# The late score matmuls issued as two instruction groups: the pooled rounds with six dense blocks a head first, the other dense blocks a few groups later

## The chip, the cores and the metric

The kernel runs on one core of one Trainium2 chip, in one launch. The metric is device time in microseconds (us). TensorE (PE) multiplies, VectorE (DVE) and ScalarE (ACT) read its results from PSUM, GpSimd (POOL) works between SBUF tensors, and SyncE (SP) issues the DMAs.

## What is computed

For 8 batches with 8 heads, 576 positions and 64 features per head, two attentions are added, and the sum goes through a token-mixing step of rank 32 and a feed-forward network (FFN) of width 2048:

```python
q_d, k_d, v_d = (t.reshape(B, H, S // 4, 4, D).mean(axis=3) for t in (q, k, v))
out_up = np.repeat(sm_attn(q_d, k_d, v_d), 4, axis=2)      # pooled: softmax over 144 x 144
mask = np.abs(pos[:, None] - pos[None, :]) < 4             # local: 7 keys for each query
scores = np.where(mask, scale * q @ k.T, -1e9)
x = out_up + softmax(scores) @ v                           # heads side by side: (B, S, 512)
u = x + (x.transpose(0, 2, 1) @ U @ V).transpose(0, 2, 1)
out = u + np.maximum(u @ w_ch1, 0.0) @ w_ch2
```

(The softmax and the transposes are shortened here.) All arithmetic is in 32 bits; the FFN splits each operand into a high and a low part (uH, uL, W1H, W1L and so on) and adds three products.

## The kernel before

**Work and names.** The FFN takes 256 steps, one for each batch, half of the positions (288) and block of 128 hidden features. A step is twelve matmuls into `ps_h` (line 888), a Relu on ACT into `hH` (L895), the rest `hL` on DVE (L896), and three steps later twelve matmuls into four `acc` tiles (L911). Below, "a group" is twelve FFN matmuls. Attention runs for two heads at a time, called a pair here. The first five pairs take an early path; the other 27 take the late path, which is where the change is. Between FFN groups a late pair puts five kinds of work on PE: the scores `ps_b` (L719 and L726), the transposes `ps_t` (L539), the weighted sums `ps_a` (L552), the mixing `ps_hu` (L848) and `ps_u` (L863).

**The scores of a late pair.** Two PSUM tiles, one for each head, are 128 partitions by 512 columns. Partitions 0 to 71 hold in columns 114 to 401 the pooled scores (`pooled_view`). The dense blocks, 32 queries by 38 keys each, are the local scores: three for each of the first three groups of 32 partitions, in columns 0 to 113, and nine for the last group, in columns 0 to 341. The function `mm` issues all 48 passes of both heads in one run: the first pooled half with three dense blocks of the last group beside it, twelve blocks of all groups, the second pooled half with the last three blocks. Passes on different groups of 32 output partitions, and on the two heads' halves of 64 input partitions, run side by side in PE's array.

**Who reads them.** The pooled part goes to a maximum `mx` on DVE (L520), its negative `nb` on ACT (L522) and four exponentials `E` on ACT (L525); then come the transposes, the sums and a store `up_s`. The dense part goes to four copies `se` on ACT (L744), a store to DRAM `s_s`, a reload `sc`, the local softmax (`ms` on DVE, L770, and what follows), the products `Pt` on POOL (L799) and their sums on DVE (L804).

**What sets the order.** All work is first recorded as operations with an engine, an assumed duration, buffers and a priority. `Plan.run` then places them in assumed time, on each engine the ready operation with the lowest priority number first, and emits the instructions in that order; each engine runs its own in order. FFN groups have numbers from 1000 up, attention work below 320, so attention goes first when the plan holds it ready. A latency `lat` is added between an operation and those that need it. Semaphore waits are added afterwards by the layer under the kernel, by buffer: for a PSUM tile, an instruction waits for the accesses by other engines to the same tile that stand ahead of it in the emitted order, whichever columns they touch. So a DVE maximum may wait for an ACT copy of the same tile, and a later PE pass into it waits for both. PSUM tiles of a late pair's scores, transposes and sums share one tag with two buffers.

**The first 236 us.** W1 and W2 are converted on the core from 64-bit to 32-bit parts, five instructions on ACT and DVE and one on POOL for each block of 512 columns (`c`, `w1r`, `w2r`, W1H, W2L; lines 341 to 354), while the FFN of batch 0 and the attention of batch 1 already run.

Of the kernel before, what the change touches and what calls it, by code (L numbers as in the profile page):

```python
# [15 lines left out]
AF = mybir.ActivationFunctionType  # L16
ALU = mybir.AluOpType
AX = mybir.AxisListType
# [3 lines left out]
PE, DVE, ACT, POOL, SP = range(5)  # L22
SLACK_FROM = 80
SLACK = 0.0
MARGIN, MARGIN_FROM = (0.5,0.0,0.0,0.0,0.0), 50
LATENCY = (0.2, 0.15, 0.2, 0.2, 0.95)


class Buf:
# [24 lines left out]
class Plan:  # L54
# [6 lines left out]
    def buf(self, pool, shape, dt, name, tag=None, bufs=1):  # L61
        return Buf(self, pool, shape, dt, name, tag or name, bufs)

    def op(self, eng, dur, fn, r=(), w=(), prio=0.0, after=(), lat=None, move=0.0, at=0.0):
        o = Op()
        o.eng, o.dur, o.fn, o.prio, o.succ, o.ndep, o.ready = eng, dur, fn, prio, [], 0, at
        o.lat, o.move = LATENCY[eng] + SLACK * (SLACK_FROM <= prio < 1000) if lat is None else lat, move
        deps = set(after)
# [133 lines left out]
def attn_mix_ffn_kernel(ctx: ExitStack, tc, q, kp, vp, qT, kT, v, U, Ub, V, w1, w2, mask, band, eye, pat, pool, vw, vn, ident, outT):  # L202
# [25 lines left out]
    QL, KL = 32, 38  # L228
# [8 lines left out]
    op, buf = plan.op, plan.buf  # L237
# [82 lines left out]
    for _ in range(2):  # L320
        m = kept_tile([NS, 2, KW], "ms_b")
        op(POOL, 0.4, lambda m=m: nc.gpsimd.tensor_copy(
            out=m()[:, :, :, KL:KW].rearrange("p r h k -> p (r h) k"),
            in_=pat_sb.unsqueeze(1).broadcast_to([128, 2 * NS, KW - KL])), ["pat"], [(m, "pat")], 0.1)
# [170 lines left out]
    def late_global(b, hp, up_s, prio):  # L495
        h0 = 2 * hp
        g = lambda shape, name, bufs=1: buf(glo, shape, F32, name, None, bufs)
        sq, sk = g([128, SD], "smq"), g([128, SD], "smk")
        qr, kr = g([128, S], "gq"), g([128, SPAD], "gT")
        load_t(qr, qT, b, h0, prio)  # L500
        load_t(kr, kT, b, h0, prio)
        pool_halves(qr, 0, sq, False, prio)
        pool_halves(kr, (SPAD - S) // 2, sk, False, prio)
        vss = []
        for hh in range(2):
            x, vs = g([QH, 2, 4, D], "vr"), g([QH, 2, D], "vs", 2)
            vss.append(vs)
            dma(lambda hh=hh, x=x: nc.sync.dma_start(
                out=x(), in_=v[b, h0 + hh].rearrange("(a p r) d -> p a r d", a=2, r=4)), [], [x], prio, 150)
            pool_tt(256, lambda x=x: nc.gpsimd.tensor_tensor(  # L510
                out=x()[:, :, 0:2, :], in0=x()[:, :, 0:2, :], in1=x()[:, :, 2:4, :], op=ALU.add), [x], [x], prio)
            pool_tt(128, lambda x=x, vs=vs: nc.gpsimd.tensor_tensor(
                out=vs(), in0=x()[:, :, 0, :], in1=x()[:, :, 1, :], op=ALU.add), [x], [vs], prio)
        s_s = buf(dram, [2, S, KL + 1], F32, "s_s", bufs=4)
        ps = late_scores(qr, kr, sq, sk, s_s, prio - 0.4)
        rs, rr, ri = (g([QH, 4], n) for n in ("rs", "rr", "ri"))
        Es = [g([QH, 2, SD], "E", 2) for _ in range(2)]
        for hh in range(2):
            mx, nb = g([QH, 2], "mx", 2), g([QH, 2], "nb", 2)
            dve(288, lambda hh=hh, mx=mx: nc.vector.tensor_reduce(  # L520
                out=mx(), in_=pooled_view(ps[hh]), axis=AX.X, op=ALU.max), [ps[hh]], [mx], prio)
            act(2, lambda mx=mx, nb=nb: nc.scalar.activation(  # L522
                nb(), mx(), AF.Copy, scale=-1.0 / 128.0), [mx], [nb], prio, 0.16)
            for a in range(2):
                act(SD, lambda a=a, hh=hh, nb=nb: nc.scalar.activation(  # L525
                    Es[hh]()[:, a, :], pooled_view(ps[hh])[:, a], AF.Exp, bias=nb()[:, a:a + 1], scale=1.0 / 128.0,
                    accum_out=rs()[:, 2 * hh + a:2 * hh + a + 1]), [ps[hh], nb], [(Es[hh], a), (rs, a, hh)], prio, 0.237)
        act(4, lambda: nc.scalar.activation(rr(), rs(), AF.Copy, bias=4e-9, scale=4.0),
            [(rs, a, hh) for a in range(2) for hh in range(2)], [rr], prio, 0.16)
        dve(24, lambda: nc.vector.reciprocal(out=ri(), in_=rr()), [rr], [ri], prio)  # L530
        ek = [(E, a) for E in Es for a in range(2)]
        view = lambda t: t()[:QH, :2 * SD].rearrange("p (c q) -> p c q", c=2)
        pt = psum_pair(ps_m, "ps_t", "m:g", 2)

        def t_mm():
            for hh in range(2):
                for c in range(2):
                    for a in range(2):
                        nc.tensor.transpose(view(pt[hh])[:, c, a * QH:(a + 1) * QH],  # L539
                                            Es[hh]()[:, a, c * QH:(c + 1) * QH], ident_sb[:QH, :QH])  # L540
        op(PE, 0.52, t_mm, ek + ["ident"], pt, prio)
        for hh in range(2):
            act(288, lambda hh=hh: nc.scalar.activation(Es[hh](), view(pt[hh]), AF.Copy),
                [pt[hh]], [(Es[hh], 0), (Es[hh], 1)], prio, 0.05)
        pa = psum(ps_m, "ps_a", "m:g", 2)
        out = lambda: pa()[:QH, :4 * D].rearrange("p (a d) -> p a d", a=4)

        def a_mm():
            for hh in range(2):
                for a in range(2):  # L550
                    for c in range(2):
                        nc.tensor.matmul(out()[:, 2 * hh + a, :], Es[hh]()[:, c, a * QH:(a + 1) * QH],  # L552
                                         vss[hh]()[:, c, :], start=(c == 0), stop=(c == 1))
        op(PE, 1.06, a_mm, ek + vss, [pa], prio)
        od = g([QH, 4, D], "od")
        dve(256, lambda: nc.vector.tensor_tensor(
            out=od(), in0=out(), in1=ri().unsqueeze(2).broadcast_to([QH, 4, D]), op=ALU.mult), [pa, ri], [od], prio)

        def store(hh):
            for a in range(2):  # L560
                nc.sync.dma_start(
                    out=up_s()[hh, a * QH * 4:(a + 1) * QH * 4, :].rearrange("(p r) d -> p r d", r=4),
                    in_=od()[:, 2 * hh + a, :].unsqueeze(1).broadcast_to([QH, 4, D]))
        for hh in range(2):
            dma(lambda hh=hh: store(hh), [od], [(up_s, hh)], prio, 160, 0.85)
        return s_s
# [143 lines left out]
    HB, LB = 3, NL - 9  # L710
    pooled_view = lambda t: t()[:QH, HB * KL:HB * KL + 2 * SD].rearrange("p (a k) -> p a k", a=2)

    def late_scores(qr, kr, sq, sk, s_s, prio):
        ps = psum_pair(ps_m, "ps_b", "m:g", 2)

        def dense(c, r):
            n = HB * c + r
            for hh, o in enumerate(heads):
                nc.tensor.matmul(ps[hh]()[c * QL:(c + 1) * QL, r * KL:(r + 1) * KL], qr()[o, n * QL:(n + 1) * QL],  # L719
                                 kr()[o, n * QL:n * QL + KL], start=True, stop=True)  # L720

        def pooled(a):
            for c in range(3):
                m = slice(c * QL, min((c + 1) * QL, QH))
                for hh, o in enumerate(heads):
                    nc.tensor.matmul(ps[hh]()[m, HB * KL + a * SD:HB * KL + (a + 1) * SD],  # L726
                                     sq()[o, a * QH + m.start:a * QH + m.stop], sk()[o], start=True, stop=True)

        def mm():
            pooled(0)  # L730
            for r in range(3):
                dense(3, r)
            for r in range(HB):
                for c in range(3):
                    dense(c, r)
                dense(3, 3 + r)
            pooled(1)
            for r in range(6, LB):
                dense(3, r)
        op(PE, 1.1, mm, [qr, kr, sq, sk], ps, prio)  # L740
        for hh in range(2):
            se = buf(loc, [128, LB, KL], F32, "se", bufs=2)
            for n, rows in ((HB, slice(0, 3 * QL)), (LB, slice(3 * QL, 4 * QL))):
                act(n * KL, lambda p=ps[hh], se=se, n=n, rows=rows: nc.scalar.activation(  # L744
                    se()[rows, 0:n].rearrange("p r k -> p (r k)"), p()[rows, 0:n * KL], AF.Copy), [ps[hh]], [(se, n)], prio)

            def put(hh=hh, se=se):
                for c in range(4):
                    n = HB if c < 3 else LB
                    to = s_s()[hh, HB * c * QL:(HB * c + n) * QL, :]  # L750
                    dst = bass.AP(tensor=to.tensor, offset=to.offset, ap=[[KL, QL], [QL * (KL + 1), n], [1, KL]])
                    nc.sync.dma_start(out=dst, in_=se()[c * QL:(c + 1) * QL, 0:n])
            dma(put, [(se, HB), (se, LB)], [(s_s, hh)], prio, 100, 1.7)
        return ps
# [296 lines left out]
```

## Time and profile before

| what | value |
|---|---|
| three runs | 1033.8, 1037.79, 1038.47 us; median 1037.79 |
| the profiled execution | 1038.36 us; its span on the core is 1036.6 us |
| mean granted TensorE clock | 0.981 |
| busy share PE, DVE, ACT, POOL | 96%, 51%, 37%, 54% |

The profiled execution is 0.57 us above the median of the three runs. 1.76 us of it lie outside the span, before the first and after the last instruction. Busy PE counts overlapping matmuls once, and their ends are modelled; so how dense PE's work is must be read from starts, not from busy time.

### The profile page before, as it was taken

To read this page: it belongs to the slowest core of one execution; us is meant where nothing else is said; L and a number is where in the kernel's file an instruction comes from. 1 tells how busy PE (TensorE), PEld (TensorE's weight loads), DVE (VectorE), ACT (ScalarE), POOL (GpSimd) and SP (SyncE) were. 2 spreads that over 40 slices of the span, in tenths; PEclk is the share of its full clock that TensorE was granted. 3 is DMA by queue.
4 is the path that set the end of the run, shared out by engine and by line. 5 is a ranking of instruction groups with operands and counts; after the bars stand their busy time and mean duration, and the time that the engine had idled before them with its cause. 6 is when DMAs were issued, how large, how long until landed. Compare 5 with 4: busy or idle time off the path is not lost.

```text
span 1036.6 us, 26946 instructions
## 1 busy us (share of the span) xinstructions
PE 996.9 (96%) x10831; PEld 975.3 (94%) x10831; DVE 529.8 (51%) x1054; ACT 388.0 (37%) x1234; POOL 557.2 (54%) x567
## 2 busy tenths in 40 slices
PE   6778898999999999999999999999999999999998
PEld 5667888999999999999999999999999999999998
DVE  5997898655554545444475344534652544211111
ACT  3676554442443434443344244423443232111110
POOL 4854568788575656565585638762765625211010
PEclk9896999999999999999999999999999999999999
DMA  8866764753555545545555355624644242000000
GB/s 279 226 172 179 199 186 116 149 138 104 135 137 115 141 113 132 128 86 146 120 137 125 87 132 133 143 75 101 151 116 117 64 113 50 24 1 24 1 24 23
DMA packets 222612, 120.30 MB, mean 116 GB/s; under 512 B 175492, under 2 KB 198456, under 8 KB 222488
## 3 DMA queue, kind: packets, MB, share of 16 engines
q1 hardware_dynamic: 222488, 118.58, 45.5%
q8 instruction: 85, 1.39, 0.6%
q14 instruction: 39, 0.32, 0.1%
HBM read 87.78 MB, written 30.75 MB: 114 GB/s over the span
## 4 chain that ended last, share of the span: by engine, by line
PE 84%; DVE 7%; POOL 3%; issue 2%; DMA 2%; ACT 2%; SPq 0%; DVEq 0%; POOLq 0%; ACTq 0%
PE acc L911 36%; PE ps_h L888 35%; PE ps_a L552 2%; PE ps_b L719 2%; DVE c L347 2%; PE ps_hu L848 1%; DVE c L349 1%; PE ps_t L539 1%; DMA w2r<-in_W 1%; PE ps_b L726 1%; POOL Pt L799 1%; DVE c L342 1%; DVE c L344 1%; PE ps_a L484 1%; PE ps_v L431 1%
## 5 line engine op out<-in xcount | busy, mean ns | idle before, releaser
L911 PE MATMUL acc<-hH,W2H 128*128 128x288 f32 x1024 | 310.5, 303 | 0.0
L896 DVE SCALAR_TENSOR_TENSOR hL<-ps_h,hH 128x288 fp32r<-128x288 f32 x256 | 116.6, 455 | 378.6 <-ACT hH L895 378.0
L888 PE MATMUL ps_h<-uH,W1H 128*128 128x288 f32 x1024 | 304.3, 297 | 4.1 <-DVE hL L896 3.1
L911 PE MATMUL acc<-hH,W2L 128*128 128x288 f32 x1024 | 303.1, 296 | 2.6 <-POOL W2L L354 2.6
L888 PE MATMUL ps_h<-uL,W1H 128*128 128x288 f32 x1024 | 303.4, 296 | 1.2 <-POOL uL L871 1.2
L911 PE MATMUL acc<-hL,W2H 128*128 128x288 f32 x1024 | 302.6, 296 | 0.0
L888 PE MATMUL ps_h<-uH,W1L 128*128 128x288 f32 x1024 | 302.0, 295 | 0.0
L799 POOL TENSOR_TENSOR Pt<-vl,at 128x896 f32<-128x896 f32 (+1 forms) x135 | 233.4, 1809 | 115.1 <-DVE acc L804 61.1
L895 ACT ACTIVATE hH<-ps_h 128x288 fp32r<-128x288 f32 x256 | 105.1, 410 | 433.6 <-PE ps_h L888 433.5
L888 PEld LDWEIGHTS ps_h<-uH,W1H 128*128 128x128 f32 x1024 | 193.5, 189 | 5.4 <-DVE hL L896 3.8
L911 PEld LDWEIGHTS acc<-hH,W2L 128*128 128x128 f32 x1024 | 193.2, 189 | 3.5 <-POOL W2L L354 3.5
L888 PEld LDWEIGHTS ps_h<-uL,W1H 128*128 128x128 f32 x1024 | 193.4, 189 | 1.5 <-POOL uL L871 1.5
L911 PEld LDWEIGHTS acc<-hH,W2H 128*128 128x128 f32 x1024 | 193.3, 189 | 1.1
L888 PEld LDWEIGHTS ps_h<-uH,W1L 128*128 128x128 f32 x1024 | 193.7, 189 | 0.0
L911 PEld LDWEIGHTS acc<-hL,W2H 128*128 128x128 f32 x1024 | 193.7, 189 | 0.0
L804 DVE TENSOR_REDUCE acc<-Pt 128x128 f32<-128x1024 f32 (+1 forms) x135 | 144.7, 1103 | 4.7 <-POOL Pt L799 2.3
L871 POOL TENSOR_TENSOR uL<-xT,uH 128x288 fp32r<-128x288 f32 x56 | 44.1, 811 | 71.3 <-ACT uH L869 71.2
L921 POOL TENSOR_TENSOR o<-uH,uL 128x288 f32<-128x288 f32 x64 | 49.8, 816 | 54.2 <-DMA out_t<-o 54.2
L840 POOL TENSOR_TENSOR xL<-xL,xH 116x640 fp32r<-116x640 f32 x28 | 44.0, 1572 | 64.2 <-ACT xH L839 49.3
L510 POOL TENSOR_TENSOR vr<-vr 72x256 f32<-72x256 f32 x54 | 42.4, 785 | 46.9 <-DMA vr<-in_v 46.8
L793 ACT ACTIVATE Pt<-ul 128x128 f32<-128x128 f32 (+1 forms) x135 | 48.4, 441 | 21.3 <-DVE acc L804 20.0
L744 ACT ACTIVATE se<-ps_b 96x114 f32<-96x114 f32 x108 | 38.5, 357 | 47.1 <-PE ps_b L719 34.1
(129 smaller groups left out, 1106.9 us busy)
## 6 DMA issues: line engine op xcount, KB each, us to landing
vl<-in_vp SPq DMA_DIRECT2D x54, 240.0 KB
out_t<-o SPq DMA_DIRECT2D x64, 144.0 KB
w1r<-in_W SPq DMA_DIRECT2D x16, 512.0 KB
w2r<-in_W SPq DMA_DIRECT2D x16, 512.0 KB
Y<-x_s SPq DMA_DIRECT2D x112, 72.0 KB
gT<-in_kT SPq DMA_DIRECT2D x27, 291.0 KB
xL<-x_s SPq DMA_DIRECT2D x28, 280.0 KB
gq<-in_qT SPq DMA_DIRECT2D x27, 288.0 KB
```

Of the source, the lines that this page charges most:

```text
L510: pool_tt(256, lambda x=x: nc.gpsimd.tensor_tensor(out=x()[:, :, 0:2, :], in0=x()[:, :, 0:2, :], in1=x()[:, :, 2:4, :], op=ALU.add), [x], ...
L744: act(n * KL, lambda p=ps[hh], se=se, n=n, rows=rows: nc.scalar.activation(se()[rows, 0:n].rearrange("p r k -> p (r k)"), p()[rows, 0:n * ...
L793: act(n * D, lambda n=n, ps=ps, Pt=Pt: nc.scalar.activation(Pt()[:, :n, :, 7], ul()[:, ps, :], AF.Copy), [ul], [(Pt, 1)], prio, 0.16)
L799: nc.gpsimd.tensor_tensor(out=Pt()[:, :n, :, 0:7].rearrange("p s d o -> p o s d"), in0=win, in1=at()[:, ps, :].rearrange("p s o -> p o s") ...
L804: dve(8.5 * n * D, lambda n=n, ps=ps, Pt=Pt: nc.vector.tensor_reduce(out=acc()[:, ps, :], in_=Pt()[:, :n], axis=AX.X, op=ALU.add), [(Pt, 0 ...
L840: pool_tt(640, lambda: nc.gpsimd.tensor_tensor(out=xL(), in0=xL().bitcast(F32), in1=xH().bitcast(F32), op=ALU.subtract), [xL, xH], [xL], prio)
L871: pool_tt(TN, lambda uH=uH, uL=uL, uf=uf: nc.gpsimd.tensor_tensor(out=uL()[:, hp, :], in0=uf(), in1=uH()[:, hp, :].bitcast(F32), op=ALU.su ...
L888: nc.tensor.matmul(ps()[:, :TN], w[:, dc, fs], u()[:, dc, :], start=(n == 0), stop=(n == 3 * NDC - 1))
L895: last_h[i] = act(TN, lambda: nc.scalar.activation(hH(), ps()[:, :TN], AF.Relu), [ps], [hH], FIRST, 0.05)
L896: dve(TN, lambda: nc.vector.scalar_tensor_tensor(hL(), ps()[:, :TN], 0.0, hH().bitcast(F32), op0=ALU.max, op1=ALU.subtract), [ps, hH], [hL ...
L911: nc.tensor.matmul(ac[e]()[:, :TN], W2[w][:, fc, es], hx(), start=(fc == 0 and n == 0), stop=(fc == NFC - 1 and n == 2))
L921: pool_tt(TN, lambda e=e, o1=o1: nc.gpsimd.tensor_tensor(out=o1()[:, :TN], in0=uH()[:, e, :].bitcast(F32), in1=uL()[:, e, :].bitcast(F32), ...
```

## The change

The 48 passes are recorded as two operations in place of one. The first, `first`, holds both pooled halves and six dense blocks of the last partition group of each head; the second, `rest`, holds the other twelve blocks of each head. `rest` needs `first` and 1.2 us (`RUN_GAP`) after it in the plan's time. The maximum and the exponentials need `first` alone; the copies `se` need both. The assumed durations add up to what they were (0.65 + 0.45 = 1.1 us). No pass is added or taken away.

```diff
+RUN_GAP = 1.2
...
-                out=mx(), in_=pooled_view(ps[hh]), axis=AX.X, op=ALU.max), [ps[hh]], [mx], prio)
+                out=mx(), in_=pooled_view(ps[hh]), axis=AX.X, op=ALU.max), [(ps[hh], 0)], [mx], prio)
...
-        def mm():
-            pooled(0)
-            for r in range(3):
-                dense(3, r)
+        def first():
+            for a in range(2):
+                pooled(a)
+                for r in range(3 * a, 3 * a + 3):
+                    dense(3, r)
+
+        def rest():
             for r in range(HB):
                 for c in range(3):
                     dense(c, r)
-                dense(3, 3 + r)
-            pooled(1)
-            for r in range(6, LB):
-                dense(3, r)
-        op(PE, 1.1, mm, [qr, kr, sq, sk], ps, prio)
+                dense(3, 6 + r)
+        op(PE, 0.65, first, [qr, kr, sq, sk], [(p, 0) for p in ps], prio, lat=RUN_GAP)
+        op(PE, 0.45, rest, [qr, kr, (ps[0], 0), (ps[1], 0)], [(p, 1) for p in ps], prio)
...
-                    se()[rows, 0:n].rearrange("p r k -> p (r k)"), p()[rows, 0:n * KL], AF.Copy), [ps[hh]], [(se, n)], prio)
+                    se()[rows, 0:n].rearrange("p r k -> p (r k)"), p()[rows, 0:n * KL], AF.Copy), [(ps[hh], 0), (ps[hh], 1)], [(se, n)], prio)
```

Because the plan places everything anew, the order changes on all engines from the first late pair on. In the emitted order PE leaves the FFN 162 times for other work, in place of 138. Ahead of the FFN's first group of batch 1 stand the scores of five late pairs, in place of six. Three places show the rest. The names in the rows are those of the code; "waits" names the engine or DMA queue whose semaphore an instruction waits for, and x29 stands for that many equal rows in a row.

First, PE at the seventh late pair, before:

```order
L911 MATMUL acc_3719<-hH,W2L 128x288
L726 MATMUL ps_b<-smk,smq 32x144 [waits DVE_49] x2
L726 MATMUL ps_b<-smk,smq 32x144 x2
L726 MATMUL ps_b<-smk,smq 8x144 x2
L719 MATMUL ps_b<-gT,gq 32x38 [waits DMAHW7_49,DMAHW0_49]
L719 MATMUL ps_b<-gT,gq 32x38 x29
L726 MATMUL ps_b<-smk,smq 32x144 x4
L726 MATMUL ps_b<-smk,smq 8x144 x2
L719 MATMUL ps_b<-gT,gq 32x38 x6
L888 MATMUL ps_h<-uH,W1H 128x288
```

And the same pair after the change, where 24 FFN matmuls (two groups) stand at the line of dots:

```order
L727 MATMUL ps_b<-smk,smq 32x144 [waits DVE_49,Pool_49]
L727 MATMUL ps_b<-smk,smq 32x144 [waits DVE_49]
L727 MATMUL ps_b<-smk,smq 32x144 x2
L727 MATMUL ps_b<-smk,smq 8x144 x2
L720 MATMUL ps_b<-gT,gq 32x38 [waits DMAHW6_49,DMAHW5_49]
L720 MATMUL ps_b<-gT,gq 32x38 x5
L727 MATMUL ps_b<-smk,smq 32x144 x4
L727 MATMUL ps_b<-smk,smq 8x144 x2
L720 MATMUL ps_b<-gT,gq 32x38 x6
...
L720 MATMUL ps_b<-gT,gq 32x38 [waits DVE_49,Activation_49] x2
L720 MATMUL ps_b<-gT,gq 32x38 x22
```

The one run of 48 passes is now two of 24, and the second starts with waits of its own, on DVE (the maximum of each tile) and on ACT (an exponential of each tile). At 14 of the 27 pairs 24 FFN matmuls stand between the two, at the others 12 to 21; at 20 pairs the second group waits for an exponential, at most others for maxima alone.

Second, ACT at the seventh late pair, before:

```order
L895 ACTIVATE hH<-ps_h 128x288 [waits PE_49]
L744 ACTIVATE se<-ps_b 96x114 [waits DMAHW4_49,DMAHW3_49,PE_49]
L744 ACTIVATE se<-ps_b 32x342 [waits DVE_49]
L744 ACTIVATE se<-ps_b 96x114 [waits DMAHW6_49,DMAHW0_49,DVE_49]
L744 ACTIVATE se<-ps_b 32x342
L522 ACTIVATE nb<-mx 72x2 x2
L895 ACTIVATE hH<-ps_h 128x288 [waits PE_49]
L525 ACTIVATE E,rs<-ps_b,nb 72x144 [waits Activation_49]
```

The same place after:

```order
L897 ACTIVATE hH<-ps_h 128x288 [waits PE_49]
L523 ACTIVATE nb<-mx 72x2 [waits DVE_49]
L526 ACTIVATE E,rs<-ps_b,nb 72x144 [waits PE_49,Activation_49]
L526 ACTIVATE E,rs<-ps_b,nb 72x144
L523 ACTIVATE nb<-mx 72x2 [waits DVE_49]
L526 ACTIVATE E,rs<-ps_b,nb 72x144 [waits PE_49,Activation_49]
L897 ACTIVATE hH<-ps_h 128x288 [waits PE_49]
L526 ACTIVATE E,rs<-ps_b,nb 72x144 [waits PE_49]
L746 ACTIVATE se<-ps_b 96x114 [waits DMAHW6_49,DMAHW7_49,DMAHW5_49,DMAHW4_49]
L746 ACTIVATE se<-ps_b 32x342
```

The copies `se`, which stood ahead of `nb` and the exponentials, now stand behind them.

Third, DVE at the first maximum of the fourth late pair, in the middle of the conversion of W2 (`c`), before:

```order
L896 SCALAR_TENSOR_TENSOR hL<-ps_h,hH 128x288 [waits Activation_49]
L349 SCALAR_TENSOR_TENSOR c_2328<-w2r,c_2328 128x512 [waits DVE_49]
L342 TENSOR_SCALAR c_2420<-c_2420 128x512 [waits Activation_49]
L772 TENSOR_REDUCE lmx<-ms 128x9
L520 TENSOR_REDUCE mx<-ps_b 72x2 [waits PE_49,Activation_49]
L344 TENSOR_SCALAR c_2420<-c_2420 128x512 [waits DVE_49]
```

After:

```order
L350 SCALAR_TENSOR_TENSOR c_2309<-w2r,c_2309 128x512 [waits DVE_49]
L898 SCALAR_TENSOR_TENSOR hL<-ps_h,hH 128x288 [waits Activation_49]
L345 TENSOR_SCALAR c_2359<-c_2359 128x512 [waits DVE_49]
L774 TENSOR_REDUCE lmx<-ms 128x9
L521 TENSOR_REDUCE mx<-ps_b 72x2 [waits PE_49]
L348 SCALAR_TENSOR_TENSOR c_2359<-w2r,c_2359 128x512 [waits DMAHW3_49,DVE_49]
```

The maximum keeps its place among the conversions, but in the changed kernel PE's second group of that pair, 24 FFN matmuls after the first, waits for it and for the exponential that follows it on ACT.

More of the change, by code (lines that the diff above doesn't have):

```diff
@@ L526, in late_global @@
                     Es[hh]()[:, a, :], pooled_view(ps[hh])[:, a], AF.Exp, bias=nb()[:, a:a + 1], scale=1.0 / 128.0,
-                    accum_out=rs()[:, 2 * hh + a:2 * hh + a + 1]), [ps[hh], nb], [(Es[hh], a), (rs, a, hh)], prio, 0.237)
+                    accum_out=rs()[:, 2 * hh + a:2 * hh + a + 1]), [(ps[hh], 0), nb], [(Es[hh], a), (rs, a, hh)], prio, 0.237)
         act(4, lambda: nc.scalar.activation(rr(), rs(), AF.Copy, bias=4e-9, scale=4.0),
```

## The prediction

> **What bounds the kernel now.** I read the page's busy shares and its chain of work first:
>
> ```profile
> span 1036.6 us, 26946 instructions
> PE 996.9 (96%) x10831; PEld 975.3 (94%) x10831; DVE 529.8 (51%) x1054; ACT 388.0 (37%) x1234; POOL 557.2 (54%) x567
> PE 84%; DVE 7%; POOL 3%; issue 2%; DMA 2%; ACT 2%; SPq 0%; DVEq 0%; POOLq 0%; ACTq 0%
> ```
>
> TensorE carries 84% of the chain, no other engine over 7%. Where the rest lies is in busy time by stretch (length, then busy time of PE, its weight loads, DVE, ACT, POOL, then the granted clock):
>
> ```profile
> 84.00:103.00 19.00, 15.79 (x334) 14.35 (x334) 16.20 (x28) 11.68 (x33) 11.10 (x10) 0.66 0.80 204
> 103.00:169.00 66.00, 57.56 (x621) 54.58 (x606) 59.96 (x103) 35.94 (x104) 41.70 (x37) 0.97 0.64 172
> 169.00:203.00 34.00, 34.00 (x354) 33.74 (x354) 21.76 (x42) 14.20 (x48) 26.44 (x25) 0.96 0.62 151
> 203.00:236.00 33.00, 31.00 (x338) 30.27 (x338) 20.85 (x42) 15.19 (x49) 28.94 (x32) 1.00 0.55 132
> 236.00:840.00 604.00, 603.54 (x6693) 598.06 (x6692) 297.09 (x604) 228.73 (x768) 369.67 (x378) 1.00 0.50 119
> 840.00:1036.00 196.00, 193.06 (x1480) 192.81 (x1479) 48.24 (x100) 33.67 (x87) 33.39 (x33) 1.00 0.10 28
> ```
>
> From 236 to 840 us PE idles 0.46 of 604 us, at full clock: whatever is added to PE there is added to the time, and an earlier softmax gains nothing. After 840 there is no late pair. Only 84 to 236 us holds idle PE time, 3.21 + 8.44 + 2.00 = 13.65 us, where DVE is busy 60 of 66 us. A shorter attention chain could gain there alone. These are the longest waits of PE in 84 to 236:
>
> ```profile
> PE ps_h L888 <- DVE hL L896: 3.1, 3, 1.4
> PE acc L911 <- POOL W2L L354: 2.6, 4, 1.0
> PE ps_hu L848 <- POOL Ust L354: 2.5, 1, 2.5
> ```
>
> They hang on conversions of weights and on DVE's order, not on scores.
>
> **The change, part by part.** *(a) The passes.* 1944 + 648 matmul instructions in 27 runs, 96 for each (two for a pass), before and after. None is added: 0.
>
> ```profile
> L719 PE MATMUL ps_b<-gT,gq x1944: 191/202/269, 84.4 to 834.5; 64*32 64x38 f32 x195
> L726 PE MATMUL ps_b<-smk,smq x648: 279/283/447, 84.4 to 834.4; 64*32 64x144 f32 x97, 64*8 64x144 f32 x65
> ```
>
> *(b) One more change of form for each pair.* PE's timeline at the seventh late pair, start and length in us, with a transposes' run behind it:
>
> ```profile
> 258.95 0.29 PE L911 MATMUL acc<-hL,W2H 128*128 128x288 f32 x1
> 259.08 0.29 PE L911 MATMUL acc<-hH,W2L 128*128 128x288 f32 x1
> 259.31 0.33 PE L726 MATMUL ps_b<-smk,smq 64*32 64x144 f32 x6
> ...
> 260.30 0.30 PE L719 MATMUL ps_b<-gT,gq 64*32 64x38 f32 x7
> 260.53 0.40 PE L888 MATMUL ps_h<-uH,W1H 128*128 128x288 f32 x1
> 260.77 0.29 PE L888 MATMUL ps_h<-uL,W1H 128*128 128x288 f32 x1
> ...
> 262.23 0.29 PE L911 MATMUL acc<-hH,W2H 128*128 128x288 f32 x1
> ...
> 263.81 0.29 PE L888 MATMUL ps_h<-uH,W1H 128*128 128x288 f32 x1
> ...
> 265.27 0.29 PE L888 MATMUL ps_h<-uH,W1L 128*128 128x288 f32 x1
> 265.40 0.66 PE L539 MATMUL ps_t<-ident_sb,E 72*72 72x72 f32 x8
> 265.87 0.38 PE L911 MATMUL acc<-hH,W2H 128*128 128x288 f32 x1
> 266.09 0.29 PE L911 MATMUL acc<-hL,W2H 128*128 128x288 f32 x1
> ```
>
> The FFN's pace is 0.132 us a matmul: twelve from 262.23 to 263.81. The score run starts 0.23 behind the last FFN matmul, 0.10 more than the pace; the transposes, whose form is 72*72 and not 64*32, start at the pace (265.40 - 265.27 = 0.13). On the way out, the last dense matmul starts at 260.41 (the row's end, 260.60, less 0.19 for one), the first FFN matmul 0.12 later, and the second FFN matmul 0.24 behind that, 0.11 over the pace. So entering and leaving costs 0.10 + 0.11 = 0.21 us at least, if the 0.12 is the last pass's own; 0.10 + 0.12 + 0.11 = 0.33 at most. I take 0.28, since a dense pass inside the run is followed by the next within 0.04 or so (seven starts in 0.11 us from 260.30), which leaves 0.08 of the 0.12. To the upper end I add 0.05, because the second pooled round no longer starts under the tail of dense blocks: 0.38. Of the 27 second groups one stands right before another run of 32-column form (an early pair's `ps_ba`), so 26 count: 26 x 0.28 = 7.3 us, between 26 x 0.21 = 5.5 and 26 x 0.38 = 9.9. Four pairs lie before 169 us, where PE waits for others anyway; of their 3 x 0.28 I take half off: 6.9.
>
> The Trainium skill ("TensorE: Matmul & The Clock Gate", Part 3, on the span model) says that a pack of tiled matmuls lasts one matmul and about 4 ns for each further tile. By it a second pack would cost one dense matmul more, 0.20 us, and the sum would be an estimated 5.3 us. The timeline shows the further 0.10 and 0.11 at the edges, so I keep the rows' price.
>
> *(c) The new wait on PE.* The second group waits for accesses of its tiles that stand ahead of it: both maxima and mostly one or two exponentials. Queued behind it is the whole FFN. What DVE and ACT need at this pair today:
>
> ```profile
> 261.04 0.82 DVE L520 TENSOR_REDUCE mx<-ps_b 72x2 f32<-72x288 f32 x2 [2.38 <-ACT se L744]
> 260.75 0.26 ACT L744 ACTIVATE se<-ps_b 96x114 f32<-96x114 f32 x1 [2.58 <-PE ps_b L719]
> 261.53 1.21 ACT L744 ACTIVATE se<-ps_b 32x342 f32<-32x342 f32 x3 [0.52 <-DVE mx L520]
> 262.77 0.30 ACT L522 ACTIVATE nb<-mx 72x2 f32<-72x2 f32 x2
> 263.09 0.41 ACT L895 ACTIVATE hH<-ps_h 128x288 fp32r<-128x288 f32 x1
> 263.40 0.37 ACT L525 ACTIVATE E<-ps_b,nb 72x144 f32<-72x144 f32 x1
> 263.75 0.37 ACT L525 ACTIVATE E<-ps_b,nb 72x144 f32<-72x144 f32 x1
> ```
>
> With the copies `se` behind instead of ahead, counted from the end of the first group: the first maximum starts 0.15 later (as 260.75 after 260.60) and is done at 0.6, the second at 0.15 + 0.82 = 0.97; `nb` 0.2, two exponentials of 0.36, the other `nb`, one more exponential, and a Relu of 0.41 between them: 0.6 + 0.2 + 0.72 + 0.2 + 0.37 + 0.41 = 2.5 us. PE arrives after 24 FFN matmuls at 24 x 0.132 + 0.1 = 3.3 us; where 12 to 18 stand between (1.7 to 2.5 us) mostly maxima alone are waited for. So 0 from the fifth pair on, with 0.8 us to spare; that cover is lost if DVE or ACT is late by more.
>
> *(d) The same wait at the fourth late pair, where they are late.* Its scores and first readers, with PE ahead:
>
> ```profile
> 152.81 0.45 PE L719 MATMUL ps_b<-gT,gq 64*32 64x38 f32 x12
> 156.90 4.02 DVE L342 TENSOR_SCALAR c<-c 128x512 f32<-128x512 f32 x1
> 160.97 0.44 DVE L520 TENSOR_REDUCE mx<-ps_b 72x2 f32<-72x288 f32 x1
> 161.68 0.38 ACT L525 ACTIVATE E<-ps_b,nb 72x144 f32<-72x144 f32 x1
> ```
>
> The run ends at 153.26, the first exponential at 162.06: 8.8 us later, and PE would arrive after 3.3, so it would stand for 5.5 us. Against that, PE's later waits in this stretch, 2.5 on `Ust` and about 1.0 on `hL`, hang on DVE and POOL work that does not wait for PE; they shrink by as much. Net +2.0, between 0 (DVE reaches the maximum in time) and 5.5 (nothing is given back). For the second pair, whose maximum stands behind `ms`, I add nothing, by the same cover.
>
> *(e) What moves.* Five score runs in place of six stand before batch 1's FFN: 1.42 us (260.77 - 259.08 - 2 x 0.132) and the transposes and sums with them are issued later, at full PE load: 0. The copies, stores `s_s` and reloads `sc` start some 4 us later on ACT and SP; what covers that is the distance to the pair's mixing, many groups later, and if it fails, `Pt` on POOL is late next. SP's queue gets no DMA more.
>
> Sum: 6.9 + 0 + 2.0 = +8.9 us on the profiled execution's 1038.36, 1047.3; it lies 0.57 above the median of the runs shown, so **1046.7 us** on their scale.
>
> **The rivals.** *Faster: the early stretch pays.* The softmax no longer queues behind 1.9 us of copies (260.75 to 262.74), so the pooled outputs of batch 1's three late pairs leave earlier, and PE's 13.65 idle us before 236 shrink. It decides from 6.9 us regained. Against it: the waits named above are for W2L, Ust and hL, and DVE has 60 of 66 us. With all idle time gone: 1037.8 + 6.9 - 13.65 = 1031. I give 0.05 to anything below 1032.6.
>
> *No change: the second change of form hides.* If loads of the next weights cover most of it, 0.1 us a pair remains, 26 x 0.1 = 2.6, and with half of (d) 1041.4. For it speaks that `ps_t` enters for nothing; against it that all score runs of the timeline show the same edges. With (b) at its low end and (d) paid back beyond its price by a better early order, it also ends near here. 0.17.
>
> *Slower by much: the wait bites at each pair.* If ACT still reaches the third exponential where it does today, 264.11 + 0.38 - 260.60 = 3.9 us behind, PE stands 0.6 at the 20 pairs that wait for exponentials: 12 us more, 1059. The Trainium skill ("PSUM — Partial Sum Buffer", on bank collisions) asks that PE and the readers of a bank and quadrant be kept apart by semaphores, so this wait could not just be left off; today's trace has no such wait on PE. Against it: the copies moved. 0.08.
>
> *The softmax gains nothing* (in pairs 1 and 3 the maximum stands behind the second group): the price (b) is paid all the same, and it gives the forecast's time.
>
> **How the numbers follow.** My forecast has 0.70, the rivals 0.05, 0.17 and 0.08. Its own range is 1037.8 + 5.5 - 0.4 = 1043 to 1037.8 + 9.9 - 0.4 + 5.5 = 1053. The range takes in most of the case without change: 1040.5 to 1053. A measurement of this kernel can tell about 0.5%, 5.2 us: faster (under 1032.6) 0.05, same 0.18, slower (over 1043.0) 0.77.
>
> **What would show it.** PE should leave the FFN 162 times, with 24 score passes in each of two runs; each second run's edges should again be 0.10, and 0.11 on the second FFN matmul after it, and the two runs of a pair together cost 1.42 + 0.28 = 1.7 us. From 236 to 840 PE should stay without idle time, and that stretch of work grow by some 6 us. A wait of `ps_b` at L720 on DVE or ACT should be seen at the fourth pair and almost nowhere else. I am wrong if the sum of both runs stays near 1.42, if such waits stand at many pairs, or if batch 1's first FFN group moves by more than 5 us.

## The result, and the profile after

The changed kernel took 1048.27 us (median of four runs, 1046.82 to 1051.81), the kernel before 1038.13 (four runs, 1033.8 to 1039.0): a ratio of 1.010, interval 1.0077 to 1.0124. It is slower by 1%, near the predicted 1046.7 and inside the range. The profiled execution took 1046.82 us, 8.46 more than that of before, at a granted clock of 0.980 (0.981 before). It is the fastest of its four, so sums from its trace are compared with 8.46 and not with the 10.1 between the medians.

From the page: the span, the busy shares, and the chain of work by engine.

```profile
span 1045.0 us, 27027 instructions
PE 1001.8 (96%) x10831; PEld 974.9 (93%) x10831; DVE 540.5 (52%) x1054; ACT 390.9 (37%) x1234; POOL 557.1 (53%) x567
PE 85%; DVE 8%; ACT 3%; DMA 2%; issue 1%; POOL 0%; SPq 0%; DVEq 0%; ACTq 0%
```

PE has the same 10831 matmuls and still carries the chain. Busy time by stretch, columns as before:

```profile
84.00:103.00 19.00, 12.73 (x283) 11.37 (x282) 18.21 (x29) 11.54 (x32) 11.84 (x10) 0.79 0.73 201
103.00:169.00 66.00, 58.59 (x655) 55.33 (x654) 62.88 (x106) 36.52 (x106) 43.24 (x38) 0.98 0.66 171
169.00:203.00 34.00, 34.00 (x358) 33.52 (x357) 21.01 (x39) 10.95 (x33) 26.68 (x24) 1.00 0.55 135
203.00:236.00 33.00, 30.49 (x239) 29.89 (x237) 20.40 (x36) 13.13 (x41) 25.81 (x27) 0.95 0.48 120
236.00:840.00 604.00, 603.49 (x6647) 593.16 (x6646) 302.73 (x605) 231.65 (x770) 369.12 (x380) 1.00 0.50 120
840.00:1044.00 204.00, 201.51 (x1627) 200.78 (x1625) 50.45 (x106) 37.98 (x104) 34.34 (x35) 1.00 0.12 31
```

From 236 to 840 us PE again idles 0.5 us of 604, but it starts 46 matmuls fewer in that time. The loss is no waiting. It lies in how PE's work follows on itself, and that is read from starts. PE's timeline at one pair, its two score runs (starts and lengths in us):

```profile
321.99 0.29 PE L890 MATMUL ps_h<-uL,W1H 128*128 128x288 f32 x1
322.12 0.29 PE L890 MATMUL ps_h<-uH,W1L 128*128 128x288 f32 x1
322.34 0.33 PE L727 MATMUL ps_b<-smk,smq 64*32 64x144 f32 x6
...
322.94 0.30 PE L720 MATMUL ps_b<-gT,gq 64*32 64x38 f32 x7
323.17 0.40 PE L913 MATMUL acc<-hH,W2H 128*128 128x288 f32 x1
323.41 0.29 PE L913 MATMUL acc<-hL,W2H 128*128 128x288 f32 x1
...
326.32 0.29 PE L890 MATMUL ps_h<-uH,W1L 128*128 128x288 f32 x1
326.54 0.64 PE L720 MATMUL ps_b<-gT,gq 64*32 64x38 f32 x48
327.12 0.40 PE L913 MATMUL acc<-hH,W2H 128*128 128x288 f32 x1
327.35 0.30 PE L913 MATMUL acc<-hL,W2H 128*128 128x288 f32 x1
```

From here on, the *cost* of a run is the time between the FFN matmul ahead of it and the second one behind it, less two FFN paces of 0.1325 us. The first run costs 323.41 - 322.12 - 0.265 = 1.02 us, the second 327.35 - 326.32 - 0.265 = 0.77. The medians over the pairs after 240 us are 1.018 and 0.770, together 1.788. Before, the one run of 48 passes cost 1.423 by the same measure. So a pair costs 0.365 more, and 26 x 0.365 = 9.5 us.

By FFN groups (of 12 matmuls), the start of group 66, with batch 1 some groups under way, comes 1.7 us earlier than before; group 128 stands at +0.2, 256 at +5.0, 389 at +8.1, 511 (the last) at +8.4. Between groups 66 and 511 the score runs grew from 30.55 us (21 pairs) to 40.13 (22 pairs), which is 9.6 of the 10.1 us by which this part is longer. One more pair at 1.8 us is in it, since it moved behind batch 1's start.

### The profile page after: what moved, and what is told of

It is laid out like the page before. It is cut to its first block, busy times and chain, and to the rows that moved or that the text cites. A ratio compares the mean times of both kernels' runs of the same rounds, so it can differ in the third digit from the quotient of the medians.

```text
span 1045.0 us, 27027 instructions
## 1 busy us (share of the span) xinstructions
PE 1001.8 (96%) x10831; PEld 974.9 (93%) x10831; DVE 540.5 (52%) x1054; ACT 390.9 (37%) x1234; POOL 557.1 (53%) x567
## 4 chain that ended last, share of the span: by engine, by line
PE 85%; DVE 8%; ACT 3%; DMA 2%; issue 1%; POOL 0%; SPq 0%; DVEq 0%; ACTq 0%
PE acc L913 37%; PE ps_h L890 36%; PE ps_a L553 2%; PE ps_b L720 2%; PE ps_hu L850 2%; DVE c L348 2%; PE ps_t L540 1%; DVE c L350 1%; DVE c L343 1%; DVE c L345 1%; PE ps_b L727 1%; PE ps_a L485 1%; PE ps_hu L678 1%; PE ps_u L865 1%; ACT E_e L460 1%
## 5 line engine op out<-in xcount | busy, mean ns | idle before, releaser
L801 POOL TENSOR_TENSOR Pt<-vl,at 128x896 f32<-128x896 f32 (+1 forms) x135 | 230.9, 1806 | 122.7 <-DVE at L784 57.3
L526 ACT ACTIVATE E<-ps_b,nb 72x144 f32<-72x144 f32 x108 | 40.0, 373 | 15.2 <-PE ps_b L720 13.7
```

Of the source, the lines that this page charges most:

```text
L526: act(SD, lambda a=a, hh=hh, nb=nb: nc.scalar.activation(Es[hh]()[:, a, :], pooled_view(ps[hh])[:, a], AF.Exp, bias=nb()[:, a:a + 1], scal ...
L801: nc.gpsimd.tensor_tensor(out=Pt()[:, :n, :, 0:7].rearrange("p s d o -> p o s d"), in0=win, in1=at()[:, ps, :].rearrange("p s o -> p o s") ...
```

## The experiments

Eleven kernels were run. Unless it says otherwise, a ratio is to the kernel before, run on the same chip beside it; it is worked out from all runs of both, so it need not be the quotient of the two medians that stand with it. Costs are medians over the pairs after 240 us.

**The new order in one run.** The passes stand in the changed order, but in one operation.

```diff
-        op(PE, 0.65, first, ..., [(p, 0) for p in ps], prio, lat=RUN_GAP)
-        op(PE, 0.45, rest, ..., [(p, 1) for p in ps], prio)
+        def whole():
+            first()
+            rest()
+        op(PE, 1.1, whole, [qr, kr, sq, sk], [(p, k) for p in ps for k in range(2)], prio)
```

> All 48 passes in one operation again, in the changed kernel's pass order; everything else stands as before. If the price is in entering and leaving PE's 64*32 form (my theory), a pair's scores cost 1.42 to 1.47 us of FFN pace, against 1.42 before and 1.02 + 0.77 = 1.79 after the change, and the time is within 1.5 us of before. If it is in the pass order (the two pooled rounds back to back), a pair costs 1.7 to 1.8 us and the time is 7 to 10 us over before.

Measured: 1039.18 us against 1039.78, ratio 1.0002 (0.9982 to 1.0022). A pair costs 1.527, 0.10 more than before. The order alone is not what makes the kernel slower: 27 x 0.10 = 2.8 us is a little over the upper end of the interval (2.3 us), so the time does not show it. The 1% needs the second run.

**Splitting only the early pairs, or only the others.** A counter lets the first four late pairs keep the old single run, or lets them alone be split.

```diff
+        count["late"] = count.get("late", 0) + 1
+        if count["late"] >= 5:      # the other kernel: <= 4
             op(PE, 0.65, first, ...); op(PE, 0.45, rest, ...)
+        else:
+            op(PE, 1.1, mm, ...)    # before's mm
```

> Split from the fifth late pair on, the first four pairs as before. Theory: 23 pairs x 0.365 us = 8.4 us over before, and the stretch up to 170 us as before. If the early waits carried the loss, it would be within 3 us of before.

> Only the first four late pairs are split, the other 23 as before. Theory: PE's wait of about 2.4 us at the fourth pair's second group is seen and is given back by 170 us; the time is within 2 us of before. Rival, that the wait stays in the time: 2.5 to 5 us over before.

Measured: split from the fifth pair on 1.0089 (1.0057 to 1.012), 1047.64 us; split up to the fourth 0.9993 (0.9974 to 1.0012), 1038.14. The loss is in the pairs from the fifth on. PE's waits of the kernel that splits the first four show the stand at the fourth pair all the same (total, times, longest):

```profile
PE ps_b L720 <- ACT E L526: 2.4, 1, 2.4
```

The time does not show those 2.4 us (the interval ends at 1.2 us over), so the early stretch gives them back: in the same list `ps_h` waits 0.8 us for `hL`, in place of 3.1, and the wait for `Ust`, 2.5 us before, is gone.

**The old order, split.** Before's order of passes, cut after 24, with the readers needing both halves. Here PE has no new wait on the softmax, and no reader starts early.

```diff
+        def one():   # pooled(0), dense(3,0..2), dense(0..2,0), dense(3,3), dense(0..1,1)
+        def two():   # the rest of mm, in its order
-        op(PE, 1.1, mm, ...)
+        op(PE, 0.65, one, ..., lat=RUN_GAP); op(PE, 0.45, two, ...)
```

> Two operations of 24 passes in the order of before (cut after the first 24), 1.2 us apart in the plan; maxima, exponentials and copies need both, so PE gets no new wait. The one-run kernel showed 1.527 us a pair for the changed pass order against 1.423, so of the change's 0.365 us a pair the order is 0.10 and the edges should be 0.26. Theory: both runs of a pair cost 1.423 + 0.26 = 1.68 us, +6.8 us over before. Rival, that the cost of a split depends on where it is cut: under 1.55 or over 1.78 us a pair.

Measured: 1.0111 (1.0082 to 1.0139), 1051.59 us against 1039.14. The runs cost 0.943 + 0.847 = 1.790, the same as the changed kernel's 1.788. PE's timeline at one pair:

```profile
299.96 0.29 PE L932 MATMUL acc<-hH,W2L 128*128 128x288 f32 x1
300.19 0.33 PE L727 MATMUL ps_b<-smk,smq 64*32 64x144 f32 x6
...
300.93 0.40 PE L932 MATMUL acc<-hH,W2H 128*128 128x288 f32 x1
301.17 0.29 PE L932 MATMUL acc<-hL,W2H 128*128 128x288 f32 x1
...
302.88 0.29 PE L909 MATMUL ps_h<-uH,W1L 128*128 128x288 f32 x1
303.11 0.31 PE L720 MATMUL ps_b<-gT,gq 64*32 64x38 f32 x20
...
303.75 0.40 PE L932 MATMUL acc<-hH,W2H 128*128 128x288 f32 x1
303.99 0.30 PE L932 MATMUL acc<-hL,W2H 128*128 128x288 f32 x1
```

So the account that I had made from the first kernel, 0.10 for the order and 0.26 for the edges, fell. A second run costs 0.37 a pair in either order, and the 0.10 of the new order was seen only where all 48 passes stand together. That is 26 x 0.37 = 9.5 of the 12.4 us measured. In its list of PE's waits two lines are longer than in the changed kernel (1.5 and 0.2 us there):

```profile
PE ps_t L540 <- ACT E L526: 5.0, 4, 3.0
PE ps_h L909 <- DVE hL L917: 2.3, 2, 1.8
```

The trace does not put the rest on the first of them. The execution profiled here took 1056.52 us, the longest of the four. At FFN group 0, ahead of the late pairs, it is 4.2 us behind the trace of before; up to group 66, where all of the first line lies, it loses 0.5 us more, and from there to group 511 another 13.4. In this last part the score runs grew by 8.8 us; near 360 us PE also stands 1.8 us for `hL`, and then works 10 us at a granted clock of 0.82 to 0.84. What the rest is in the other three executions stays open.

**A second run of almost nothing.** 46 passes in the first run, the last dense block of each head in the second; the gap in the plan and the readers are those of the changed kernel.

```diff
+        def most():  # mm with range(6, LB - 1) in its last loop
+        def last():
+            dense(3, LB - 1)
```

> The order of before, but the last dense block alone (two passes, one for each head) is cut off as a second run. The price of an edge by itself: theory 0.30 us for the second run (edges 0.26 and the two passes), and 1.40 for the first. If a second run is priced by its passes, it costs under 0.1 us.

Measured: 1047.12 us in a single execution, so without an interval (1039.14 before); by its trace the runs cost 1.402 + 0.391. Two passes still cost 0.39 us. PE's timeline of one such second run:

```profile
327.02 0.29 PE L904 MATMUL ps_h<-uL,W1H 128*128 128x288 f32 x1
327.15 0.29 PE L904 MATMUL ps_h<-uH,W1L 128*128 128x288 f32 x1
327.38 0.26 PE L720 MATMUL ps_b<-gT,gq 64*32 64x38 f32 x4
327.57 0.41 PE L927 MATMUL acc<-hH,W2H 128*128 128x288 f32 x1
327.81 0.29 PE L927 MATMUL acc<-hL,W2H 128*128 128x288 f32 x1
```

The run starts 0.23 behind the FFN matmul, where the pace is 0.13. The first FFN matmul starts 0.19 behind the run's start, the second 0.24 behind the first. The four instructions start within 0.07 (0.26 less 0.19 for one), so the last of them starts 0.12 ahead of the FFN. By the rows 0.10 + 0.12 + 0.11 = 0.33 of the 0.39 is entering and leaving. The Trainium skill ("TensorE: Matmul & The Clock Gate", Part 3) gives a pack of tiled matmuls one matmul's time and some 4 ns for each further tile: an estimated 0.20 us here, from the 0.19 of a dense matmul. The trace has 0.26 us for the four instructions themselves, and 0.39, about twice the estimate, for what they take from the FFN. The Trainium skill's page "TensorEngine Tiling (Array Packing)", Key Properties, says that a change of tiling mode drains TensorE, and names no price. That such a drain is what the 0.33 us go to would fit, but no run here shows it.

**Three runs.** The second group cut into 12 and 12 passes, groups of the FFN between.

```diff
-        op(PE, 0.45, rest, ...)
+        op(PE, 0.25, rest, ..., lat=RUN_GAP)   # 12 passes
+        op(PE, 0.2, third, ...)                # the other 12
```

> The second group of the changed kernel cut once more, into two of 12 passes, so that PE leaves the FFN three times for a pair's scores. Three cuts so far (24/24 in the changed order, 24/24 in the order of before, 46/2) all gave 1.79 us a pair against 1.42 in one run: 0.37 us for a second run, wherever it is cut. Theory: that price is per run, so a pair costs 1.42 + 2 x 0.37 = 2.16 us, 2 x 26 x 0.37 = 19 us over before. Rival, that a third run of small passes is nearly free because the form was used a few us ago: 1.8 us and about 9 us over before.

Measured: 1056.09 us against 1036.8, ratio 1.0191 (1.0164 to 1.0218), as far up as expected, but a pair costs only 1.019 + 2 x 0.473 = 1.965, 0.54 over one run instead of two full steps of 0.37. 27 x 0.54 = 14.6 of the 19.3 us; new early waits stand beside it. PE's waits of this kernel:

```profile
PE ps_u L873 <- DVE stk L863: 3.8, 1, 3.8
PE ps_hu L858 <- DVE acc L814: 3.7, 1, 3.7
```

So the total came out as expected partly by luck: the edges cost less than I had put down, and the early waits more. The price of a dense run is not a constant and a price for each pass: 2 passes cost 0.39, 12 cost 0.47, 24 cost 0.77. Between 2 and 12 a pass adds 8 ns, from 12 to 24 it adds 25. Two runs of 12 (0.95) cost only 0.18 more than one of 24.

**The second group right behind the first.** This takes away the FFN work that stands between the two.

```diff
-        op(PE, 0.65, first, ..., lat=RUN_GAP)
+        op(PE, 0.65, first, ..., lat=-0.6)
```

> Two operations as in the changed kernel, but the second with no gap in the plan, so that it stands right behind the first on PE at all 27 pairs; maxima and exponentials still need the first alone in the plan. Theory of the edges: a pair costs 1.42 to 1.47 us and the time is within 2.5 us of before (the early order differs). Rival, that the new order on ACT and DVE costs the time: it stays 6 us or more above before.

Measured: 1.0265 (1.0233 to 1.0298), 1067.75 us against 1039.78, the slowest of all; I had expected it near the time before. The latency moves the maxima too, so these came ahead of the second group in the emitted order, and PE waited for them. PE's timeline at one pair, and its waits:

```profile
317.61 0.33 PE L727 MATMUL ps_b<-smk,smq 64*32 64x144 f32 x6
...
318.21 0.30 PE L720 MATMUL ps_b<-gT,gq 64*32 64x38 f32 x7
319.14 0.99 PE L720 MATMUL ps_b<-gT,gq 64*32 64x38 f32 x48 [0.64 <-DVE mx L521]
320.06 0.40 PE L913 MATMUL acc<-hH,W2H 128*128 128x288 f32 x1
```

```profile
PE ps_b L720 <- DVE mx L521: 14.5, 25, 0.7
```

A pair costs 2.57 in the mean, against 1.455 before: 27 x 1.11 = 30 us, near the 28.0 measured. The experiment says nothing on the edges, for which it was made. It shows what the changed kernel would pay without its cover: the wait for the maxima alone is worth about three times the edges.

**A shorter gap.** `RUN_GAP = 0.2` in place of 1.2, so that at 13 pairs only 6 FFN matmuls stand between the groups.

> The changed kernel with 0.2 us in place of 1.2 in the plan between the two groups: 6 FFN matmuls stand between them at 13 pairs, 12 to 15 at the others, and the second group still waits for maxima and some exponentials. After 6 matmuls PE arrives at 0.9 us, when the second maximum (0.97 by the prediction's working) is just not done, and where an exponential is waited for (1.2 us) it is not. Theory of the wait's cover: waits of 0.1 to 0.7 us at those 13 pairs, 3 to 8 us in sum, and the time 11 to 18 us over before. If the wait costs nothing even here, it is as the changed kernel, 8 to 10 us over.

Measured: 1.0111 (1.0074 to 1.0149), 1047.45 us against 1036.8. The second run costs 0.771 as the median and 0.810 as the mean; the waits that I expected did not come (0.0 to 0.08 us each, one of 0.43, and one of 1.5 at 131 us). For the maxima, six FFN matmuls and the entry (6 x 0.13 + 0.2 = 1.0 us) are cover enough there: I had counted 0.97 us until the second maximum is done, under (c), and by the trace PE starts the second group 1.11 us behind the last pass of the first, and the second maximum is just done then (1.11 to 1.16) or comes only later and is not waited for. This says nothing on the exponentials: at these pairs the first of them starts 1.8 us or more behind that pass, when the second group is already running.

**Other orders in one run.** Three attempts to keep one run and gain from the order: the dense blocks of all groups first and the pooled rounds last; pooled and dense passes in three turns that use all four partition groups at once; and dense turns and pooled rounds by turns.

```diff
+  dense first:  for r: dense(0..3, r);  for a: pooled(a), dense(3, 3a+3..3a+5)
+  rotated:      three turns of two pooled blocks, dense(c2, 0..2) and dense(3, ·)
+  alternate:    for r: dense(0..2, r), dense(3, 3r); after r < 2: pooled(r), dense(3, 3r+1..3r+2)
```

> One run with the dense rounds first and the two pooled rounds at the end. If two pooled rounds back to back cost 0.10 us a pair, as in the one-run kernel, this costs 1.52 too and the time is 0 to 3 us over before; if the cost is the dense rounds being last, it costs 1.42 or less.

> One run in which, in each of three turns, two of the first three partition groups do pooled passes while the third and the last do dense blocks. If pooled passes (long streams) and dense blocks (many weight loads) can hide each other, a pair costs 1.2 to 1.35 us and the time falls by 2 to 6 us under before; if starts in order hold them back, it costs 1.45 or more.

> One run of 48 passes with the dense rounds apart: eight dense passes, the first pooled round, eight dense, the second pooled round, eight dense, the last group's other blocks between. Runs alone cost 0.39 us for 2 dense passes, 0.47 for 12 and 0.77 for 24, so dense passes seem to run dry between the 12th and the 24th. If that is so within a run of 48 too, a pair costs 1.2 to 1.35 us and the time falls 2 to 6 us under before; if each turn from pooled to dense passes costs its own 0.1 us, a pair costs 1.45 to 1.65 us and the time is 0 to 6 us over before.

Measured: 0.999 (0.9971 to 1.001), 1.0014 (1.0 to 1.0027) and 1.0018 (0.9995 to 1.004), with 1.421, 1.530 and 1.534 us a pair. None gains. Two lose the same 0.10 as the changed order in one run. The dense-first run costs 1.42, as its expectation had it for the case that dense rounds are dear when they come last: of all five orders in one run, the two that cost 1.42 end with a pooled round and blocks of the last group, and the three that cost 1.53 end with rounds that hold dense blocks of the first three groups. No run takes this further. No version beat the kernel before.

## Why the prediction was right

**(a) The passes: right.** Their count is the same, and no run of 48 passes, in any order, was cheaper than before's by more than 0.002 us.

**(b) One more change of form: the mechanism right, the size too small.** PE leaves the FFN 161 times by the trace, 137 before, and each second run has its edges. The step that was mis-sized is the one that takes 0.04 off the 0.12 between the last pass and the FFN and keeps 0.08 (0.10 + 0.08 + 0.11 = 0.29, put down as 0.28); measured are 0.365 a pair, near the upper end of 0.38. The parts: the run starts 0.224 behind the FFN (0.09 over pace), the second FFN matmul 0.238 behind the first (0.11 over), and the FFN follows the last pass by 0.13, nearly all of it extra: the run of two passes pays it too. That makes 0.33, the most that I gave the edges. The further 0.03 to 0.04 lie inside the runs: from the first start of a run to its last there are 1.10 us before, 0.70 + 0.44 after, and 0.61 + 0.52 with the old order split. Why is not settled: the 0.05 that I added for the loss of overlap between pooled rounds and dense blocks has the size, but the old order pays 0.37 too, which speaks against that reason. Between groups 66 and 511 (b) came to 22 x 0.365 = 8.0 us, where I had 22 x 0.28 = 6.2.

**(c) The new wait from the fifth pair on: right, at 0.** The second runs cost 0.807 us in the mean and 0.770 as the median: 22 x 0.04 = 0.8 us in all, nearly all of it at two pairs. PE's waits from 236 to 840 us have one line:

```profile
PE ps_b L720 <- ACT E L526: 0.4, 1, 0.4
```

The cover is real: without it the wait for the maxima costs some 1.1 us a pair (the second group right behind the first), but 6 FFN matmuls in place of 24 still cover that (the shorter gap). At two pairs of that kernel with 12 FFN matmuls between, two exponentials end 1.78 us behind the last pass and PE arrives at 1.92 to 1.93; the second run costs 0.78 to 0.79 there, so by these times 12 cover the exponentials too.

**(d) The fourth pair: the wait is there, its size and its price were both too large.** PE:

```profile
157.93 0.29 PE L890 MATMUL ps_h<-uH,W1L 128*128 128x288 f32 x1
160.63 0.64 PE L720 MATMUL ps_b<-gT,gq 64*32 64x38 f32 x48 [2.41 <-ACT E L526]
161.20 0.40 PE L913 MATMUL acc<-hH,W2H 128*128 128x288 f32 x1
```

DVE and ACT there:

```profile
156.97 2.02 DVE L345 TENSOR_SCALAR c<-c 128x512 int32<-128x512 int32 x1
...
159.04 0.44 DVE L521 TENSOR_REDUCE mx<-ps_b 72x2 f32<-72x288 f32 x1
```

```profile
159.51 0.20 ACT L523 ACTIVATE nb<-mx 72x2 f32<-72x2 f32 x1 [1.58 <-DVE mx L521]
159.75 0.38 ACT L526 ACTIVATE E<-ps_b,nb 72x144 f32<-72x144 f32 x1
...
160.12 0.36 ACT L526 ACTIVATE E<-ps_b,nb 72x144 f32<-72x144 f32 x1
```

Another conversion stands ahead of the maximum: it lasts 2.02 us, where the one in before's row lasted 4.02. The wait was 2.4 and not 5.5. The 2.0 that I left of it were not lost at all: with 0.4 for the edges of the early pairs my working makes 2.4 us for splitting the first four, and the kernel that does it is at most 1.2 us over before. PE's later waits in 84 to 236 us, which hung on DVE and POOL, shrank as foretold:

```profile
PE ps_b L720 <- ACT E L526: 2.4, 1, 2.4
PE ps_u L865 <- DVE stk L855: 2.3, 1, 2.3
PE ps_b L727 <- POOL smk L418: 2.0, 1, 2.0
...
PE acc L913 <- POOL W2L L355: 1.3, 3, 0.5
...
PE ps_hu L850 <- POOL Ust L355: 0.7, 1, 0.7
...
PE ps_h L890 <- DVE hL L898: 0.2, 1, 0.2
```

`Ust` went from 2.5 to 0.7, `hL` from 3.1 to 0.2, `W2L` from 2.6 to 1.3, while `stk` (2.3) and `smk` (2.0) are the new long ones. PE's idle time in 84 to 236 grew from 13.65 to 16.2 us, yet the FFN is 1.7 us ahead at group 66, since a pair's scores, with the transposes and sums behind them (1.42 + 0.55 + 1.09 = 3.1 us by their medians), now come later. So my working had 22 x 0.28 + 1.42 = 7.6 us behind group 66, where 10.1 came, and 8.9 - 7.6 = +1.3 ahead of it, where -1.7 came. The total is right because errors of 2.5 and 3.0 us oppose each other, and that is luck. Of the 2.5, 1.8 are the size of (b). The 3.0 are not sharp: one trace is held against one, and the four kernels that keep before's order of work on PE (the runs of 48 passes in other orders) differ from before's trace by -2.5 to +1.6 us between groups 0 and 66, where the changed kernel differs by -2.1.

**(e) What moves: right.** Five score runs stand ahead of batch 1's FFN in place of six, and the sixth is found again behind it. The later copies, stores and reloads made no wait: the line under (c) is the only one from 236 to 840.

**The rivals.** The early stretch gave nothing to the total that the interval can tell (splitting the first four pairs: 0.9993, from 2.7 us under before to 1.2 over). The second change of form does not hide: even two passes pay 0.39. The wait does not bite at each pair in this kernel, though it did where the FFN work between was taken away.

## What to carry to other kernels

Where PE carries the time without a gap, splitting a run of tiled passes buys its readers an earlier start and costs PE a second entry and exit, here 0.37 us of the FFN's time, and a run of two passes pays as much. Price it from starts: from the matmul ahead of a run to the second one behind it, less the pace. And before a reader is placed ahead of a later write into the same PSUM tile, count what else the writing engine can do meanwhile: for the maxima 6 FFN matmuls were enough here, none cost 1.1 us a pair.

## What the hardware showed that I had not expected

- Not every second run has this price. PE's runs of other shapes (116*64 and 72*72 in the rows) hardly pay for being split: `ps_hu` (0.654 us) and `ps_a` (1.088) apart cost 1.742 by the same measure in the kernel before, merged into one run (three times) 1.694, so 0.05 for a second run.
- Dense passes in a run do not cost the same throughout: 0.39 us for 2, 0.47 for 12, 0.77 for 24. In the changed kernel's second runs (24 passes, 48 instructions) the starts come some 6 ns apart up to the 32nd instruction, pause there for 66 and 36 ns, and then come 11 ns apart in the mean. What in PE does that stays open.
- The order of the same 48 passes matters in one run: before's order and the dense blocks first cost 1.42 us, the three others 1.53; that the pooled rounds stand together or apart does not decide it. Split in two, before's order and the changed one cost the same. Why is open too.
